# Stage C and the first batch's stage A on 64x64 quarters of TensorE, the combination's sums on VectorE, and a thinner hand-out of Fourier work in the first batch

## The chip, the cores and the metric

The kernel runs on one core of one Trainium2 chip. The core has five engines that work side by side: TensorE (PE in the profile, with its weight loads as PEld), VectorE (DVE), ScalarE (ACT), GpSimd (POOL) and SyncE (SP), which issues most of the DMAs. The metric is the time of one execution on the device in microseconds, the median of three runs.

## What is computed

Two things follow one another for 8 batches of 3008 rows with 256 columns.

```python
X = np.fft.rfft(x, axis=1)                       # along the 3008 rows
Yr = Xr @ w_r - Xi @ w_i + b_r                   # 256 x 256, complex
Yi = Xr @ w_i + Xi @ w_r + b_i
Yr = np.sign(Yr) * np.maximum(np.abs(Yr) - 0.01, 0)   # and the same for Yi
y = np.fft.irfft(Yr + 1j * Yi, n=3008, axis=1)
h = y.reshape(24064, 256) @ w_in                 # 256 x 2048
out = (h * np.cos(h)) @ w_out                    # 2048 x 256
```

## The kernel before

3008 is 64 x 47, so each transform is made of a 64-point one and a 47-point one, both as small matrix products. For a batch the Fourier part has these steps: **stage A** (the 64-point transform, `stage_a0` L410 for batch 0, `stage_a` L432 for the others), **stage B** (`stage_b` L522: the 47-point transform `forward` L557, the combination `combine` L581 that makes the three operands of a complex product, the product with the weights `wmix` L642, the soft threshold, and the inverse 47-point transform `inverse` L747), and **stage C** (`stage_c` L861, the inverse 64-point transform). Between them the data go through scratch tensors in DRAM (`scr1`, `scrF`, `scrT`, `scr2`), which turn them.

Behind it stands the second part, `moe_step` (L912) and `second` (L894), for six tiles of 512 rows (the last has 448) a batch and 16 steps a tile: `h` in six matmuls of 512 columns into a PSUM bank `ph` (L919 to L921; all large operands are split into a high part and a rest, so that three matmuls make one product), then ACT L928, DVE L929, ACT L931, DVE L932 for `u` = h cos h, ACT L934 for its high part `gh`, and the rest `gl` on POOL (L323, two steps in four) or DVE (L326). Three steps later six matmuls into `po` (L901, L902, L905) add up the product with `w_out`.

The Fourier part of batch b+1 is written as generators and is handed out between the steps of batch b. Every `yield` names a cost in units, and before and after the `po` matmuls of a step `pull` (L1046) takes pieces until the step's budget is used: `(C_COST + share(b)) / 15 / 2`. `share` (L1035) is the sum of the costs of a batch over 6 - SPREAD tiles, for batch 0 over 6 - 0.7 = 5.3, with `HEAD`, in which START, BT_WAIT and FIRST stand, added. START is the wait before the first loads of stage B of batch 1, FIRST the rest behind its first `forward`. At the head of each tile's pieces stands stage C of the next tile: loads of `bt`, a rest of BT_WAIT units, the matmuls, and a rest of BT_REST units. Before the whole loop runs a prologue (`first` L798), in which batch 0 goes through stages A and B alone.

Instructions are put in order per engine by a scheduler that follows a timeline of its own. `tc.issue_after(x)` forbids it to place an instruction before x. `floor()` (L315) does so for the last instructions of the step before the present one.

A matmul in single precision appears in the trace as two, each with a weight load of its own, and so does a call on a quarter. `burst` (L361) issues calls that use parts of the array of 64 x 64 (or 32 x 32) in one piece: the first call waits for everything, and the rest follow it without anything between them. Four calls that follow one another there take the four quarters: two halves of the input partitions, g, and two halves of the output partitions, v, with a PSUM bank for each g. So stage A of batches 1 to 7, `forward` and `spread` are made. Stage C and `stage_a0` use the whole array instead: 128 partitions hold two groups of 64 points, and their constants (`f1` and `ei` in `ff`, columns 0 to 127 and 128 to 255) are block-diagonal, so that each group meets its own block and the other block is zero.

- `stage_a0` (L410): six pieces of `x` are loaded, each 512 KB; for each half of a piece 4 calls of 128 columns write one bank, which ACT and DVE copy by turns.
- `stage_c` (L861): a tile has two halves `hf`; for each, 4 calls of 128 columns write one bank `pc`, ACT writes the high part `xTh` and DVE the rest `xTl`.
- `combine` (L581): for each part, ACT casts `Xh` (L592, L600, L607), DVE makes the rest `Xl` (L326, L593 and L602 call it), POOL adds the two parts of `z` (L599) and makes the last rest (L323).
- `stage_a(1)` runs its first three pieces in the prologue. The stores of the pieces 1 and 2 are held back (`held`, `release` L461) until the first matmuls `pc`.

## Time and profile before

| | us |
|---|---|
| median of 3 runs (2640.57 to 2641.7) | 2640.63 |
| the profiled execution's own time | 2643.39 |
| its span, first to last instruction | 2641.6 |
| TensorE busy in it | 2603.2 |
| VectorE, ScalarE, GpSimd busy | 1937.9, 1635.1, 979.1 |

The mean granted clock of TensorE is 0.995 of full. In the profile, a group of instructions is named by its line and engine, then the tile that it writes, an arrow and the tiles that it reads. "Idle before" is the time in which the engine had nothing to run just before an instruction, and the name behind it is what ended that. The end of a matmul is modelled, and matmuls overlap in the array, so that their pitch, from start to start, is what counts.

### The profile page before, as it was taken

The numbers are of one execution on the slowest core, as the hardware profiler recorded it, in microseconds if no ns is written. First come the engines' busy times: TensorE is split into PE (matmuls) and PEld (weight loads), VectorE is DVE, ScalarE is ACT, GpSimd is POOL, SyncE is SP. The second block draws the span as 40 slices with busy tenths as digits, with TensorE's granted clock in tenths as the row PEclk, the third lists the DMA queues.
The fourth block names the chain that finished last, engine by engine and source line by source line (L and its number), as shares of the span: only waits on it lengthen the run. The fifth ranks groups of instructions, "written<-read, shape, count | busy, mean of one in ns | idle before, by whom it ended". The sixth has DMA issues, their size and how long they took to land.

```text
span 2641.6 us, 38292 instructions
## 1 busy us (share of the span) xinstructions
PE 2603.2 (99%) x13657; PEld 2112.5 (80%) x13657; DVE 1937.9 (73%) x3089; ACT 1635.1 (62%) x3003; POOL 979.1 (37%) x946
## 2 busy tenths in 40 slices
PE   9899999999999999999999999999999999999999
PEld 7478778877788777887788877887778888888888
DVE  5797677878768777687776777677776778766665
ACT  5565556666666666656666666666666666566665
POOL 1224442444425453244533455234432433322222
PEclk9999999999999999999999999999999999999999
DMA  6535434344333444244433544235433343210000
GB/s 209 186 94 150 131 116 129 97 139 137 103 88 107 140 128 116 79 125 137 140 86 86 156 140 116 85 98 143 131 99 101 86 115 108 59 46 17 17 25 16
DMA packets 172935, 282.82 MB, mean 107 GB/s; under 512 B 15608, under 2 KB 114200, under 8 KB 169160
## 3 DMA queue, kind: packets, MB, share of 16 engines
q1 hardware_dynamic: 161896, 243.78, 32.8%
q0 software_dynamic: 10112, 35.53, 4.3%
q8 instruction: 108, 1.77, 0.3%
q10 hardware_dynamic: 736, 1.05, 0.1%
q14 instruction: 83, 0.68, 0.1%
HBM read 149.76 MB, written 130.55 MB: 106 GB/s over the span
## 4 chain that ended last, share of the span: by engine, by line
PE 88%; DVE 7%; ACT 2%; DMA 2%; issue 1%; POOL 1%; SPq 0%; ACTq 0%; DVEq 0%; POOLq 0%
PE ph L919 12%; PE po L901 12%; PE po L905 12%; PE po L902 12%; PE ph L920 12%; PE ph L921 12%; PE pc L881 3%; PE pw L658 2%; PE pw L659 2%; PE pw L660 2%; PE pb L375 1%; PE pw L654 1%; DVE u L932 1%; DVE u L929 1%; DVE Xl L326 1%
## 5 line engine op out<-in xcount | busy, mean ns | idle before, releaser
L323 POOL TENSOR_TENSOR gl<-u,gh 128x512 fp32r<-128x512 f32 (+1 forms) x384 | 502.6, 1309 | 1156.2 <-ACT gh L934 983.4
L931 ACT ACTIVATE u<-u 128x512 f32<-128x512 f32 (+1 forms) x768 | 478.6, 623 | 384.9 <-DVE u L929 383.7
L929 DVE SCALAR_TENSOR_TENSOR u<-ph,u 128x512 f32<-128x512 f32 (+1 forms) x768 | 514.5, 672 | 259.0 <-ACT u L928 257.8
L932 DVE TENSOR_TENSOR u<-ph,u 128x512 f32<-128x512 f32 (+1 forms) x768 | 518.1, 675 | 237.4 <-ACT u L931 226.7
L928 ACT ACTIVATE u<-ph 128x512 int32<-128x512 f32 (+1 forms) x768 | 448.0, 585 | 280.7 <-PE ph L921 271.2
L901 PE MATMUL po<-gh,wout 128*128 128x512 f32 (+1 forms) x1536 | 606.8, 395 | 13.3 <-ACT gh L934 13.1
L934 ACT CAST gh<-u 128x512 fp32r<-128x512 f32 (+1 forms) x768 | 467.9, 609 | 244.8 <-DVE u L932 241.1
L919 PE MATMUL ph<-xTh,win 128*128 128x512 f32 (+1 forms) x1536 | 606.7, 395 | 1.1 <-ACT xTh L886 0.7
L902 PE MATMUL po<-gh,wout 128*128 128x512 f32 (+1 forms) x1536 | 602.1, 392 | 0.0
L920 PE MATMUL ph<-xTl,win 128*128 128x512 f32 (+1 forms) x1536 | 597.3, 389 | 0.0
L921 PE MATMUL ph<-xTh,win 128*128 128x512 f32 (+1 forms) x1536 | 596.1, 388 | 0.0
L905 PE MATMUL po<-gl,wout 128*128 128x512 f32 (+1 forms) x1536 | 480.7, 391 | 0.5 <-POOL gl L323 0.5
L919 PEld LDWEIGHTS ph<-xTh,win 128*128 128x128 f32 x1536 | 289.6, 189 | 90.8 <-issue 20.8
L901 PEld LDWEIGHTS po<-gh,wout 128*128 128x128 f32 x1536 | 289.8, 189 | 79.7 <-ACT gh L934 18.6
L326 DVE TENSOR_TENSOR gl<-u,gh 128x512 fp32r<-128x512 f32 (+1 forms) x384 | 295.6, 770 | 66.9 <-ACT gh L934 59.0
L905 PEld LDWEIGHTS po<-gl,wout 128*128 128x128 f32 x1536 | 288.1, 189 | 66.9 <-issue 5.3
L921 PEld LDWEIGHTS ph<-xTh,win 128*128 128x128 f32 x1536 | 289.6, 189 | 57.5
L902 PEld LDWEIGHTS po<-gh,wout 128*128 128x128 f32 x1536 | 289.8, 189 | 54.6
L920 PEld LDWEIGHTS ph<-xTl,win 128*128 128x128 f32 x1536 | 289.8, 189 | 50.7 <-DVE xTl L887 0.4
L658 PE MATMUL pw<-Xh,wf 128*128 128x384 f32 x336 | 114.9, 342 | 2.0 <-ACT Xh L607 1.9
L659 PE MATMUL pw<-Xh,wf 128*128 128x384 f32 x336 | 114.0, 339 | 0.0
L660 PE MATMUL pw<-Xl,wf 128*128 128x384 f32 x336 | 111.8, 338 | 0.0
(121 smaller groups left out, 2468.5 us busy)
## 6 DMA issues: line engine op xcount, KB each, us to landing
scrF<-at SPq DMA_DIRECT2D x28, 1024.0 KB
z<-scrF SPq DMA_DIRECT2D x112, 256.0 KB
scrT<-tr SPq DMA_DIRECT2D x56, 512.0 KB
y<-scrT SPq DMA_DIRECT2D x112, 256.0 KB
bt<-scr SPq DMA_DIRECT2D x94, 256.0 KB
scr<-ao SPq DMA_DIRECT2D x84, 256.0 KB
scr<-bo SPq DMA_DIRECT2D x224, 96.0 KB
out_dram<-ob SPq DMA_DIRECT2D x80, 256.0 KB
```

What stands on the lines that cost most here:

```text
L323: return nc.gpsimd.tensor_tensor(out=lo, in0=x, in1=hi.bitcast(F32), op=ALU.subtract)
L901: mm(po[e][:, :n], wo[0][:, 0, f, es], gh[:, :n], start=f == 0, stop=False)
L902: mm(po[e][:, :n], wo[0][:, 1, f, es], gh[:, :n], start=False, stop=False)
L905: mm(po[e][:, :n], wo[0][:, 0, f, es], gl[:, :n], start=False, stop=f == NFC - 1)
L919: mm(h, win[:, 0, c, fs], th[:, c, :n], start=c == 0, stop=False)
L920: mm(h, win[:, 0, c, fs], tl[:, c, :n], start=False, stop=False)
L921: ins = mm(h, win[:, 1, c, fs], th[:, c, :n], start=False, stop=c == 1)
L928: nc.scalar.activation(k[:, :n], h, AF.Identity, bias=0.25, scale=1.0 / TWO_PI)
L929: nc.vector.scalar_tensor_tensor(out=u[:, :n], in0=h, scalar=1.0 / TWO_PI, in1=k[:, :n], op0=ALU.mult, op1=ALU.subtract)
L931: nc.scalar.activation(u[:, :n], u[:, :n], AF.Sin, bias=HALF_PI, scale=TWO_PI)
L932: product = nc.vector.tensor_tensor(out=u[:, :n], in0=h, in1=u[:, :n], op=ALU.mult)
L934: step = [nc.scalar.copy(gh[:, :n], u[:, :n])]
```

## The change

Stage C makes the same sums with 32 calls of 64 x 64 weights and 64 columns for a tile, one bank for each g, as one `burst` that waits for the loads of `bt`; the copies then go by g and no longer by half. The second tile of batch 0 rests 2.5 x BT_WAIT units between loads and matmuls. `stage_a0` makes its sums likewise, with 32 calls for a whole piece of `x`, kept together by the new `pinned`. In `combine` the sum of the parts of `z` is made by DVE instead of POOL, behind ACT's cast in the text; for batch 1 the three DVE operations have `floor(1)`, which names the last step instead of the one before. START is 6 instead of 12 and FIRST 24 instead of 36. In `stage_a(1)` the store of piece 0 is held back too.

```diff
@@ -46,7 +46,7 @@
 QUIET, READ, BURST, LAST = 3.0, 1.1, 2.5, 21.0
 BT_WAIT, BT_REST = 8.0, 2.0
 SPREAD, SPREAD_FIRST = 1.15, 0.7
-START, FIRST = 12.0, 36.0
+START, FIRST = 6.0, 24.0
 
 
 class Hold(float):
@@ -312,10 +312,10 @@
     mm = nc.tensor.matmul
     steps = []
 
-    def floor():
+    def floor(n=2):
 
         ctx = ExitStack()
-        for ins in steps[-2] if len(steps) > 1 else ():
+        for ins in steps[-n] if len(steps) > 1 else ():
             ctx.enter_context(tc.issue_after(ins.ins))
         return ctx
 
@@ -375,6 +375,12 @@
                 ins = mm(*a, **k)
         return ins
 
+    def pinned(calls):
+        ins = mm(*calls[0][0], **calls[0][1])
+        with tc.high_priority(), tc.issue_after(ins.ins):
+            for a, k in calls[1:]:
+                mm(*a, **k)
+
     def stage_out(name):
         return wk.tile([128, 1024], F32, tag="ao", name=name, bufs=3)
 
@@ -419,15 +425,17 @@
         load_fourier_w()
         load_f0(2)
         landed("x0", xs[5][:, :1])
-        for n in range(12):
-            p = fps("pa")
-            for c in range(2):
-                for i in range(2):
-                    o, k = 256 * c + 128 * i, 512 * (n % 2) + 256 * i + 128 * c
-                    mm(p[:, o:o + 128], xs[n // 2][:, k:k + 128], ff[:, :128], start=o == 0, stop=o == 384,
-                       skip_group_check=True)
-            mark["dve"] = mark["a0", n % 2] = (nc.vector.tensor_copy if n % 2 else nc.scalar.copy)(
-                a0[0][:, :, 2 * n:2 * n + 2], p.rearrange("p (c i k) -> p c i k", c=2, i=2))
+        for n in range(6):
+            p = [fps("pa") for _ in range(2)]
+            pinned([((p[g][64 * v:64 * v + 64, 256 * c + 64 * i:256 * c + 64 * i + 64],
+                      xs[n][64 * g:64 * g + 64, 256 * i + 128 * c + 64 * v:256 * i + 128 * c + 64 * v + 64],
+                      ff[64 * g:64 * g + 64, :128].rearrange("p (r g s) -> p g r s", r=2, g=2)[:, g]),
+                     dict(start=c == 0 and i == 0, stop=c == 1 and i == 3, skip_group_check=True))
+                    for i in range(4) for c in range(2) for v in range(2) for g in range(2)])
+            for g in range(2):
+                mark["dve"] = mark["a0", g] = (nc.vector.tensor_copy if g else nc.scalar.copy)(
+                    a0[0][:, :, 4 * n:4 * n + 4].rearrange("p c i (r g s) -> p g c i r s", r=2, g=2)[:, g],
+                    p[g].rearrange("p (c i r s) -> p c i r s", c=2, i=4, r=2))
 
     def stage_a(b):
         scr1[b] = dr.tile([2, 24, 32, 2, 256], F32, tag="scr1", name=f"scr1_{b}")
@@ -484,7 +492,7 @@
                     drained(p[c, h], nc.scalar.copy(ao[:, 512 * h:512 * h + 512], p[c, h]))
                     if h == 0 or c < cs[-1]:
                         yield Hold(READ)
-                if pro and c:
+                if pro:
                     held.append((c, ao))
                 else:
                     store(c, ao)
@@ -591,15 +599,16 @@
                 with floor():
                     nc.scalar.copy(hi[0][:, v], z[:, 0, v])
                 yield 0.8
-                with floor():
+                with floor(1 if b == 1 else 2):
                     rest(lo[0][:, v], z[:, 0, v], hi[0][:, v])
                 yield 0.9
             for v in range(2):
                 with floor():
-                    nc.gpsimd.tensor_tensor(out=z[:, 0, v], in0=z[:, 0, v], in1=z[:, 1, v], op=ALU.add)
                     nc.scalar.copy(hi[1][:, v], z[:, 1, v])
+                with floor(1 if b == 1 else 2):
+                    nc.vector.tensor_tensor(out=z[:, 0, v], in0=z[:, 0, v], in1=z[:, 1, v], op=ALU.add)
                 yield 0.9
-                with floor():
+                with floor(1 if b == 1 else 2):
                     rest(lo[1][:, v], z[:, 1, v], hi[1][:, v])
                 yield 1.2
             for v in range(2):
@@ -865,26 +874,28 @@
 
         bt = wk.tile([128, 4, 256], F32, tag="bt", name="bt", bufs=1)
         first = b == 0 and t == 0
+        loads = []
         for h in range(0, 4, 2 if first else 4):
             m = 2 if first else 4
             for g in range(2):
                 n0 = 24 * g + 4 * t + h
-                ((nc.scalar, nc.gpsimd)[g] if first else nc.sync).dma_start(
-                    bt[64 * g:64 * g + 64, h:h + m], scr2[b][n0:n0 + m].rearrange("i r s d -> (r s) i d"))
-        yield BT_WAIT
-        for hf in range(2):
-            p = fps("pc")
-            with tc.issue_after(mark["pa"].ins) if b == 0 and t == 0 else floor() if b == 0 and t == 1 else ExitStack():
-                for j in range(2):
-                    for c in range(2):
-                        o = 256 * j + 128 * c
-                        ins = mm(p[:, o:o + 128], bt[:, 2 * hf + j, 128 * c:128 * c + 128], ff[:, 128:256], start=o == 0, stop=o == 384,
-                                 skip_group_check=True)
-            mark.setdefault("pc", ins)
-            pv = p.rearrange("p (j c n) -> p c j n", j=2, c=2)
-            thv, tlv = (a[:, :, 256 * hf:256 * hf + 256].rearrange("p c (j n) -> p c j n", j=2) for a in (th, tl))
+                loads.append(((nc.scalar, nc.gpsimd)[g] if first else nc.sync).dma_start(
+                    bt[64 * g:64 * g + 64, h:h + m], scr2[b][n0:n0 + m].rearrange("i r s d -> (r s) i d")))
+        yield 2.5 * BT_WAIT if b == 0 and t == 1 else BT_WAIT
+        p = [fps("pc") for _ in range(2)]
+        with tc.issue_after(mark["pa"].ins) if b == 0 and t == 0 else floor() if b == 0 and t == 1 else ExitStack():
+            ins = burst(2, [((p[g][64 * v:64 * v + 64, 256 * c + 64 * i:256 * c + 64 * i + 64],
+                              bt[64 * g:64 * g + 64, i, 128 * c + 64 * v:128 * c + 64 * v + 64],
+                              ff[64 * g:64 * g + 64, 128 + 64 * g:192 + 64 * g]),
+                             dict(start=c == 0 and i == 0, stop=c == 1 and i == 3, skip_group_check=True))
+                            for i in range(4) for c in range(2) for v in range(2) for g in range(2)],
+                        () if first else loads)
+        mark.setdefault("pc", ins)
+        for g in range(2):
+            pv = p[g].rearrange("p (c i m) -> p c i m", c=2, i=4)
+            thv, tlv = (a.rearrange("p c (i g m) -> p g c i m", i=4, g=2)[:, g] for a in (th, tl))
             nc.scalar.copy(thv, pv)
-            drained(p, nc.vector.tensor_tensor(out=tlv, in0=pv, in1=thv.bitcast(F32), op=ALU.subtract))
+            drained(p[g], nc.vector.tensor_tensor(out=tlv, in0=pv, in1=thv.bitcast(F32), op=ALU.subtract))
         yield BT_REST
 
 
```

## Rows read from the trace of the kernel before

**Rows 1.** The profile's page: busy time of each engine, its share of the span and its instructions; and, from another part, the chain of work that ended last, by engine.

```profile
PE 2603.2 (99%) x13657; PEld 2112.5 (80%) x13657; DVE 1937.9 (73%) x3089; ACT 1635.1 (62%) x3003; POOL 979.1 (37%) x946
...
PE 88%; DVE 7%; ACT 2%; DMA 2%; issue 1%; POOL 1%; SPq 0%; ACTq 0%; DVEq 0%; POOLq 0%
```

**Rows 2.** Who TensorE waited for, over the whole span: the waiting engine and line, what it waited for, us in total, times, the longest.

```profile
PE po L901 <- ACT gh L934: 13.1, 8, 4.8
...
PE pw L658 <- ACT Xh L607: 1.9, 5, 0.4
```

**Rows 3.** The same view from 130 to 440 us.

```profile
PE po L901 <- ACT gh L934: 12.4, 6, 4.8
PE pc L881 <- DVE u L932: 1.8, 1, 1.8
PE pc L881 <- DMA bt<-scr: 1.7, 1, 1.7
PE pi L365 <- DMA y<-scrT: 1.3, 1, 1.3
```

**Rows 4.** Busy time by stretch: from and to in us, length, then for PE, PEld, DVE, ACT and POOL the busy us and (instructions), then the granted clock, the DMA share and GB/s.

```profile
130.00:160.00 30.00, 26.11 (x134) 20.46 (x135) 28.13 (x47) 18.77 (x34) 6.82 (x6) 0.94 0.35 95
...
280.00:300.00 20.00, 15.15 (x56) 12.22 (x56) 15.54 (x24) 11.20 (x22) 10.45 (x9) 0.83 0.35 90
...
340.00:360.00 20.00, 15.77 (x61) 12.69 (x60) 18.67 (x27) 10.31 (x21) 11.27 (x10) 0.83 0.24 74
```

**Rows 5.** Groups of instructions of one shape over the whole span: count, busy us, mean ns of one, idle us before them.

```profile
L881 PE MATMUL pc<-ff,bt 128*128 128x128 f32 x768 | 100.0, 278 | 7.2 <-DMA bt<-scr 5.4 <-DVE u L932 1.8
```

**Rows 6.** TensorE's timeline around one tile of stage C: start in us, how long the row lasts, line, output and inputs, instructions in the row.

```profile
957.48 1.95 PE L881 MATMUL pc<-ff,bt 128*128 128x128 f32 x16
959.18 0.47 PE L919 MATMUL ph<-xTh,win 128*128 128x512 f32 x1
959.50 0.39 PE L920 MATMUL ph<-xTl,win 128*128 128x512 f32 x1
959.73 0.40 PE L921 MATMUL ph<-xTh,win 128*128 128x512 f32 x1
```

**Rows 7.** TensorE's timeline around one burst of stage B on quarters.

```profile
608.58 0.40 PE L902 MATMUL po<-gh,wout 128*128 128x512 f32 x1
608.91 0.43 PE L365 MATMUL pb<-at,fq 48*64 48x256 f32 x1
...
609.18 0.38 PE L365 MATMUL pb<-at,fq 48*64 48x256 f32 x1
609.18 1.68 PE L375 MATMUL pb<-at,fq 48*64 48x256 f32 x27
610.80 0.50 PE L919 MATMUL ph<-xTh,win 128*128 128x512 f32 x1
611.14 0.40 PE L920 MATMUL ph<-xTl,win 128*128 128x512 f32 x1
```

**Rows 8.** The weight loads at the head of that burst.

```profile
608.91 0.13 PEld L365 LDWEIGHTS pb<-at,fq 48*64 48x64 f32 x1 [0.37 <-DVE u L932]
...
608.96 0.13 PEld L365 LDWEIGHTS pb<-at,fq 48*64 48x64 f32 x1
```

**Rows 9.** Busy time by stretch of TensorE alone (us, (instructions), clock, DMA share, GB/s), for the first 0.15 us of a burst of the inverse that came after a wait of 1.26 us for its data.

```profile
417.39:417.54 0.15, 0.12 (x16) 1.00 0.00 0
```

**Rows 10.** Groups of one shape again: the combination's rests on DVE, the last subtraction of the threshold on DVE, and the sums on POOL.

```profile
L326 DVE TENSOR_TENSOR Xl<-z,Xh 128x384 fp32r<-128x384 f32 x112 | 104.5, 962 | 8.9 <-ACT Xh L592 6.4 <-ACT Xh L600 2.1
...
L684 DVE TENSOR_TENSOR st<-st,cl 128x384 f32<-128x384 f32 x122 | 83.3, 686 | 1.2
...
L599 POOL TENSOR_TENSOR z<-z 128x384 f32<-128x384 f32 x56 | 69.5, 1255 | 24.8 <-DVE Xl L326 24.8
```

**Rows 11.** DVE's timeline around the long stall of batch 0 (in brackets the idle time before a row and what ended it).

```profile
273.99 0.45 DVE L715 STREAM_TRANSPOSE tr<-odd 128x256 f32<-128x256 f32 x1 [5.90 <-POOL odd L707]
...
281.88 1.45 DVE L326 TENSOR_TENSOR Xl<-z,Xh 128x384 fp32r<-128x384 f32 x1
283.25 0.54 DVE L684 TENSOR_TENSOR st<-st,cl 128x384 f32<-128x384 f32 x1
```

**Rows 12.** POOL's timeline before and in it.

```profile
266.85 1.59 POOL L448 TENSOR_TENSOR xe<-xt 128x512 f32<-128x512 f32 x1 [4.20 <-DMA xt<-in_dram]
...
271.13 1.29 POOL L449 TENSOR_TENSOR xt<-xt 128x512 f32<-128x512 f32 x1
...
283.41 1.25 POOL L599 TENSOR_TENSOR z<-z 128x384 f32<-128x384 f32 x1 [0.49 <-DVE Xl L326]
...
285.48 1.33 POOL L599 TENSOR_TENSOR z<-z 128x384 f32<-128x384 f32 x1
```

**Rows 13.** The first 20 us by stretch, columns as in rows 4.

```profile
0.00:20.00 20.00, 15.97 (x103) 14.57 (x103) 4.54 (x7) 5.00 (x8) 6.82 (x18) 0.91 0.89 262
```

**Rows 14.** The timelines of the start, one row each of TensorE, POOL and DVE.

```profile
6.75 12.61 PE L427 MATMUL pa<-ff,x 128*128 128x128 f32 x96 [1.95 <-DMA ff<-in_dram]
...
17.14 0.19 POOL L403 COPY seen<-x 128x1 f32<-128x1 f32 x1 [9.97 <-DMA ws<-in_dram]
...
19.40 0.69 DVE L429 COPY a<-pa 128x512 f32<-128x512 f32 x1 [1.09 <-PE pa L427]
```

**Rows 15.** The chain of work that ended last, from 100 to 115 us: start, us, what.

```profile
105.52 3.73 DMA bt<-scr
```

## The prediction

> **What bounds the kernel now.** I read the page's engine table and its chain of waits first. TensorE is busy 2603 of 2641.6 us and the chain runs through it for 88% of the span; DVE has 73% and POOL 37% [rows 1]. Then I read who TensorE waits for: 13.1 us for the cast `gh`, and, once in most batches, some tenths for `Xh`, 1.9 us in all [rows 2]. So after the start TensorE works almost without a pause, and only work taken from it shortens the span. [...] Batch 0 thus has 17.2 + 8.6 = 25.8 us that are no PE work.
>
> **Stage C (48 tiles).** Now: 8 calls, which the profile shows as 768 / 48 = 16 matmuls of 128 columns [rows 5]. In a tile that lies between plain matmuls the 16 start at 957.48 and the next one at 959.18, and that one holds the array 0.32 us where its kind takes 0.23 [rows 6]: 1.70 + 0.09 = 1.79 us, a pitch near 0.111. Half of what each multiplies are the zeros of the block-diagonal `ei`.
>
> After: 32 calls on 64x64 quarters, 64 matmuls of 64 columns in 16 groups of four. The nearest rows are the bursts that already run on quarters. Stage B's has 16 calls, 32 matmuls of 256 columns, 8 groups [rows 7]. Its second group starts at 609.18, and from there 1 + 27 matmuls, seven groups, last until 609.18 + 1.68 = 610.86; less the 0.38 of the last, six group steps took 1.28 us after the offset of 0.02 within a group: 0.214 each. Four quarters truly run together. Around the burst, the mode costs time: the plain matmul before started at 608.58 and should hold 0.23, but the burst starts at 608.91 (0.10 lost); the first group takes 0.27, not 0.214 (0.05: its weights load uncovered); the last group should be done at 610.68, the next plain matmul starts at 610.80 and holds 0.34 instead of 0.23 (0.12 + 0.11). Together 0.38, I take 0.37 a burst.
>
> The pitch of a group at 64 columns no row shows. From below: a quarter's second weights load 608.96 - 608.91 = 0.05 us after its first [rows 8]; and 64 columns at the pace of rows 6 are 0.111 / 2 = 0.056, as is what the first group of rows 7 is longer. From above: no gain from halving the columns, 0.111. [...] Issuing is no limit either: after a wait that had emptied the queue, 16 quarter calls started within 0.15 us [rows 9], 0.009 each; stage C wants one per 0.029.
>
> So a tile costs 16 x 0.058 + 0.37 = 1.30 us against 1.79: 0.49 saved. The first tile hangs on DMA; 47 x 0.49 = 23.0 us. With 0.05 it is 29, with 0.075 it is 10.
>
> The copies out of PSUM stay two on ACT and two on DVE a tile, but both banks now end together. Nothing waits for them, a tile being transformed long before its first `ph`; only at the very first tile do ACT's two copies follow one another where one ran beside the second half's matmuls: -0.5 to +0.6 us, nothing taken.
>
> [...]
>
> **The combination's sums.** 56 additions of 1.255 us leave POOL (70 us) and go to DVE. What one takes there no row shows; 128x384 with two SBUF operands takes DVE 0.686 on average (`st`) and 0.962 (`Xl`) [rows 10], so 38 to 54 us; I take 0.69, as for the same kind without a cast. DVE rises to about 75%. While a POOL sum runs, an `Xl` on DVE takes 1.45 us, where the similar `st` takes 0.54 [rows 11]; that goes. So for each sum DVE has 0.69 more and up to 0.9 less: nothing in the steady batches, where TensorE covers it. Queued behind the sum on DVE are `u` L929 and L932; `gh` waits for these, and `po` for `gh`. If that cover is thin, one step in each of seven batches comes 0.7 late: +5 us. If `Xh` comes earlier, the 1.9 us of rows 2 go: -2.
>
> **The first batch.** Four edits act here. START and FIRST leave 18 units fewer to hand out, so share(0) falls by 18 / 5.3 = 3.4 units and the work comes about 5% thinner; `bt` of the second tile gets 20 units to land, not 8; the sums leave POOL; DVE's part of the combination stays behind the last step, not the one before. The long stall shows what they meet: `xt` lands late, POOL works through four `xe`/`xt` operations from 266.85 on [rows 12] before it makes `odd`; DVE stands 5.90 us at `tr`, which waits for that `odd` [rows 11]; two POOL sums (1.25 and 1.33) then delay the next half's `odd` [rows 12]; DVE works off a backlog, and `po` gets `gh` 4.8 us late [rows 3]. The sums' 2.6 us go from that stall and from the like one near 355 (TensorE busy 15.77 of 20 us [rows 4]): 5.2. One of the two clock losses goes with it: 3.4. The wait for `bt`, 1.7 [rows 3], goes by the longer rest. The sums cost DVE some 1 us of it. I take 9 of the 25.8. Bounds: all of it gone, or 8 us more, if the new order makes one more stall with its clock loss (4.8 + 3.4).
>
> **The start.** The mean clock is 0.91 of full over the first 20 us [rows 13]. Stage A of batch 0 has 96 matmuls from 6.75 to 19.36 and its last copy from 19.40 to 20.09 [rows 14]; as quarters it has 96 groups x 0.058 = 5.6 us of work. But POOL's `seen`, which waits for the last piece of `x`, runs only at 17.14 [rows 14] (the row names `ws`, but by the code it is the piece of `x` that it reads); only then can the sixth burst start: 17.14 + 0.93 + 0.2 (last matmul to copy, as now) + 0.69 = 18.96, 1.1 us earlier. [...] I take 0; bounds -1.1 and +2. Stage A(1)'s first store now waits for the first `pc`: its two DMAs are no longer in flight beside the 3.73 us of `bt` [rows 15], up to 0.7 sooner. Later, the second tile's loads stand behind two more issues on SP, with 20 units to spare. Nothing taken.
>
> **Sum.** The profiled execution took 2643.39 us, 1.8 outside the span of 2641.6. 2643.4 - 23.0 - 9 = 2611.4. The median of the three runs, 2640.63, is 2.8 below the profiled one: 2608.6.
>
> **Rivals.**
> 1. Stage C gains, batch 0 doesn't: the stalls only move, since DVE is busy 28.13 of 30 us there [rows 4] and gets more to do. 2640.6 - 23 = 2617.6; with one new stall, 2626. For it: that DVE load. Against: in the long stall DVE itself was waiting for POOL.
> 2. Slower: in a quarter the load isn't hidden. Place: every stage C burst. Price: a group takes load and matmul, 0.056 + 0.058 = 0.114, a tile 16 x 0.114 + 0.37 = 2.19, 0.40 more than now; 47 of them +18.8, less 9: 2650. It decides from a pitch of (1.79 - 0.37) / 16 = 0.089 on for stage C, and of 0.10 for the whole change. [...] Against: rows 7, and the plain pitch of rows 6.
> 3. All stalls of batch 0 go: 2640.6 - 23 - 25.8 = 2592.
> 4. The pitch comes near 0.089, so the quarters give nothing: batch 0's part alone or not even that, 2632 to 2641.
>
> **How the numbers follow.** Forecast 0.62; rival 1 0.20; rival 2 0.06; rival 3 0.08; rival 4 0.04. Two tenths of a per cent, 5.3 us, is about what a measurement of this kernel can tell from no change. Faster: 0.62 + 0.20 + 0.08 + half of rival 4 = 0.92; same 0.02; slower 0.06. Range 2594 to 2627: down to pitch 0.05 with two thirds of batch 0's loss gone, up to rival 1 with its new stall.
>
> **What would show it.** Right: `pc` as 3072 matmuls, and about 1.30 us from the first of a tile to the next plain one, switches included; PE busy down by some 23 us; waits for `gh` between 130 and 440 us under 8 us; no dip of the clock in at least one of 280 to 300 and 340 to 360. Wrong: groups of four more than 0.07 apart; a wait of `po` for `gh` in every batch after 480 us; the clock down behind stage A at the start; `pc` of the second tile waiting for `bt` again.

## The result, and the profile after

The changed kernel takes 2664.94 us (2662.49 to 2667.44) where the kernel before took 2641.16 on the same chip: 1.0088 of it, with an interval of 1.0076 to 1.0101, so 23.8 us slower where 32 us faster had been forecast. The profiled execution took 2662.49 us, 1.8 outside its span.

The page of the changed kernel, the lines that answer to [rows 1]:

```profile
span 2660.7 us, 43519 instructions
PE 2590.4 (97%) x16249; PEld 2069.3 (78%) x16249; DVE 1945.2 (73%) x3145; ACT 1632.5 (61%) x3003; POOL 912.3 (34%) x890
...
PE 83%; DVE 10%; ACT 3%; DMA 2%; issue 2%; POOL 0%; SPq 0%; DVEq 0%; ACTq 0%; POOLq 0%
```

TensorE is busy 12.8 us less, but the span is 19.1 us longer: it has less to do and waits more. DVE's total hardly moved (1937.9 to 1945.2 us), yet its share of the chain rose from 7% to 10%: VectorE is not fuller, it stands in the way at more places.

Where the 19.1 us came from I read off TensorE's timeline, from one batch's first `po` to the next. Before, the first `po` of batch 1 came at 478.3 us, after at 486.5: +8.2. Batches 1 to 5 took 318.1, 317.3, 317.8, 317.5 and 319.5 us, and now 322.9, 320.0, 321.3, 320.3 and 322.6: +16.9. Batch 6, which has no stage A of a later batch beside it, went from 308.5 to 305.0, and the rest from 264.6 to 262.2: -5.9. So stage C's saving of 6 x 0.49 = 2.9 us a batch shows only at the end, where least is handed out beside the second part.

TensorE's waits from 480 us on, first of the kernel before, then of the changed one (who waited, for whom, us in total, times, the longest):

```profile
PE pw L658 <- ACT Xh L607: 1.9, 5, 0.4
PE po L901 <- ACT gh L934: 0.7, 2, 0.4
```

```profile
PE po L912 <- ACT gh L945: 15.5, 14, 2.2
PE ph L930 <- DVE u L943: 4.8, 6, 1.4
PE pw L667 <- DVE u L943: 1.6, 5, 0.3
PE po L916 <- POOL gl L323: 0.9, 5, 0.2
```

`po` almost never waited for `gh` in these batches; now it does 14 times. The longest, 2.2 us, comes once in each of the batches 1 to 5, in the fourth tile, where the combination runs. In four of the five a spell of 3.41 us at 0.50 of the full clock goes with it: behind 991.6 us, in batch 2, the mean granted clock is 0.59 until 995.7, 1.7 us lost. In batches 1 to 5 TensorE's waits thus rose from 2.6 to 22.8 us and the clock's loss from 0 to 6.8, while stage C has some 15 us less to do; that leaves 4 or 5 of the 16.9 us open.

The stretches of batch 0 that [rows 4] show, and the one behind stage A of the start, after the change (columns as there):

```profile
130.00:160.00 30.00, 25.04 (x162) 18.70 (x155) 29.16 (x43) 18.39 (x34) 10.59 (x8) 0.94 0.57 174
280.00:300.00 20.00, 19.25 (x113) 14.74 (x112) 15.91 (x25) 8.76 (x16) 11.62 (x10) 1.00 0.42 141
340.00:360.00 20.00, 20.00 (x117) 15.76 (x116) 14.23 (x22) 11.04 (x21) 10.52 (x10) 1.00 0.49 144
...
20.00:40.00 20.00, 17.12 (x131) 14.93 (x131) 7.40 (x16) 10.10 (x22) 2.10 (x4) 0.76 0.69 256
```

The two stalls near 290 and 355 us are gone, with their clock losses. But others have come. Three of TensorE's four largest waits from 130 to 440 us, after the change:

```profile
PE pi L365 <- DMA y<-scrT: 5.4, 1, 5.4
...
PE po L912 <- ACT gh L945: 4.5, 5, 2.2
PE pb L365 <- issue: 3.9, 1, 3.9
```

All waits there add up to 23.4 us (18.1 before). With the `pi` that waits for `y` until 431.05 and the `pb` that stops until 206.1 go spells at 0.50 of the full clock too, from 429.1 to 435.9 and from 207.2 to 210.7 us; the clock's loss between 130 and 440 us is 6.8 us (8.5 before). So the stalls of batch 0 moved.

From 20 to 40 us the mean granted clock is 0.76, where it was 1.00 before: 20 x 0.24 = 4.8 us lost. Over the first 20 us it is 0.99, where it was 0.91 [rows 13]; over both together the start loses 3.4 us more than before.

TensorE's timeline around one tile of stage C, which answers to [rows 6]:

```profile
970.66 0.63 PE L916 MATMUL po<-gl,wout 128*128 128x512 f32 x2
971.22 0.27 PE L365 MATMUL pc<-ff,bt 64*64 64x64 f32 x1
...
971.33 1.05 PE L375 MATMUL pc<-ff,bt 64*64 64x64 f32 x59
972.31 0.50 PE L930 MATMUL ph<-xTh,win 128*128 128x512 f32 x1
972.64 0.40 PE L931 MATMUL ph<-xTl,win 128*128 128x512 f32 x1
```

The two `po` hold 0.46 us, so the burst starts 0.10 late; it is 1.09 to the next `ph`, which holds 0.33 where its kind takes 0.23. Together 1.29 us, forecast 1.30. This part of the prediction was right, and it gained nothing in batches 1 to 5.

VectorE in the fourth tile of batch 2, in the changed kernel (start, us, what), ahead of a wait of 2.20 us that TensorE ends at 991.61:

```profile
985.85 0.67 DVE L326 TENSOR_TENSOR gl<-u,gh 128x512 fp32r<-128x512 f32 x1
986.44 0.55 DVE L326 TENSOR_TENSOR Xl<-z,Xh 128x384 fp32r<-128x384 f32 x1
986.91 0.55 DVE L609 TENSOR_TENSOR z<-z 128x384 f32<-128x384 f32 x1
987.38 2.93 DVE L326 TENSOR_TENSOR Xl<-z,Xh 128x384 fp32r<-128x384 f32 x2
990.23 0.68 DVE L943 TENSOR_TENSOR u<-ph,u 128x512 f32<-128x512 f32 x1
```

The same place in the kernel before:

```profile
973.01 2.32 DVE L326 TENSOR_TENSOR Xl<-z,Xh 128x384 fp32r<-128x384 f32 x3
975.26 0.68 DVE L932 TENSOR_TENSOR u<-ph,u 128x512 f32<-128x512 f32 x1
```

`u` now stands behind four instructions of the combination, 990.23 - 986.44 = 3.79 us; before, behind three, 975.26 - 973.01 = 2.25 us. The sum itself takes 0.55 us here (0.62 on average over all 56), less than the 0.69 that I took; the two `Xl` behind it take 1.46 each.

That is 1.5 us more, and the wait is 2.2: TensorE's own order has changed there too. The wait in the changed kernel, and the same `po`, of the sixth step of the fourth tile, in the kernel before, each with the `ph` nearest to it:

```profile
991.61 0.50 PE L912 MATMUL po<-gh,wout 128*128 128x512 f32 x1 [2.20 <-ACT gh L945]
...
993.57 0.63 PE L930 MATMUL ph<-xTh,win 128*128 128x512 f32 x1
```

```profile
980.02 0.39 PE L921 MATMUL ph<-xTh,win 128*128 128x512 f32 x1
...
982.01 0.39 PE L901 MATMUL po<-gh,wout 128*128 128x512 f32 x1
```

Before, this `po` stood behind the `ph` of two more steps and the `pw` between them, and its `gh` had ended 5.4 us ahead of it. Now it stands ahead of them, right behind the `po` of the step before. It is so in each of the batches 1 to 5.

And the start: TensorE in stage A of batch 0, two rows of the changed kernel (in brackets the idle time before; "issue" means that nothing which the profile shows held it):

```profile
14.72 0.81 PE L382 MATMUL pa<-ff,x 64*64 64x64 f32 x41 [1.90 <-issue]
...
22.01 1.24 PE L382 MATMUL pa<-ff,x 64*64 64x64 f32 x37 [5.20 <-issue]
```

Both stops lie inside a burst, whose first call had already waited for its piece of `x`. Nothing of the kind stood in [rows 14].

### The profile page after: what moved, and what is told of

Its sections match the earlier page's. It is cut to its first block, busy times and chain, and to the rows that moved or that the text cites. A ratio compares the mean times of both kernels' runs of the same rounds, so it can differ in the third digit from the quotient of the medians.

```text
span 2660.7 us, 43519 instructions
## 1 busy us (share of the span) xinstructions
PE 2590.4 (97%) x16249; PEld 2069.3 (78%) x16249; DVE 1945.2 (73%) x3145; ACT 1632.5 (61%) x3003; POOL 912.3 (34%) x890
## 4 chain that ended last, share of the span: by engine, by line
PE 83%; DVE 10%; ACT 3%; DMA 2%; issue 2%; POOL 0%; SPq 0%; DVEq 0%; ACTq 0%; POOLq 0%
PE ph L930 12%; PE po L912 12%; PE po L913 11%; PE ph L931 11%; PE ph L932 11%; PE po L916 11%; PE pw L667 2%; PE pw L668 2%; PE pw L669 2%; DVE u L943 2%; DVE u L940 1%; DVE Xl L326 1%; PE pc L375 1%; PE pb L375 1%; PE pw L663 1%
## 5 line engine op out<-in xcount | busy, mean ns | idle before, releaser
L943 DVE TENSOR_TENSOR u<-ph,u 128x512 f32<-128x512 f32 (+1 forms) x768 | 517.8, 675 | 237.5 <-ACT u L942 225.1
L939 ACT ACTIVATE u<-ph 128x512 int32<-128x512 f32 (+1 forms) x768 | 449.0, 587 | 328.5 <-PE ph L932 316.1
L930 PE MATMUL ph<-xTh,win 128*128 128x512 f32 (+1 forms) x1536 | 606.0, 395 | 10.6 <-DVE u L943 9.3
L931 PE MATMUL ph<-xTl,win 128*128 128x512 f32 (+1 forms) x1536 | 597.9, 389 | 0.1
L930 PEld LDWEIGHTS ph<-xTh,win 128*128 128x128 f32 x1536 | 290.3, 189 | 101.9 <-DVE u L943 19.1
L326 DVE TENSOR_TENSOR gl<-u,gh 128x512 fp32r<-128x512 f32 (+1 forms) x384 | 287.4, 748 | 72.8 <-ACT gh L945 68.8
L931 PEld LDWEIGHTS ph<-xTl,win 128*128 128x128 f32 x1536 | 290.5, 189 | 51.6 <-DVE xTl L898 0.6
L716 POOL TENSOR_TENSOR odd<-st 128x184 f32<-128x184 f32 (+1 forms) x112 | 69.2, 619 | 137.9 <-DVE st L693 135.2
```

The lines of the kernel that those rows point to most:

```text
L930: mm(h, win[:, 0, c, fs], th[:, c, :n], start=c == 0, stop=False)
L931: mm(h, win[:, 0, c, fs], tl[:, c, :n], start=False, stop=False)
L939: nc.scalar.activation(k[:, :n], h, AF.Identity, bias=0.25, scale=1.0 / TWO_PI)
L943: product = nc.vector.tensor_tensor(out=u[:, :n], in0=h, in1=u[:, :n], op=ALU.mult)
```

## The experiments

Three theories stood at first. S: the sums on VectorE make `gh` late. F: stage A on quarters makes the start late. B: stage C's saving is lost because TensorE, faster there, meets work that is no faster.

**e1_sum_pool: the sums back on POOL.**

```diff
-nc.vector.tensor_tensor(out=z[:, 0, v], in0=z[:, 0, v], in1=z[:, 1, v], op=ALU.add)
+nc.gpsimd.tensor_tensor(out=z[:, 0, v], in0=z[:, 0, v], in1=z[:, 1, v], op=ALU.add)
```

> The changed kernel with one edit: the combination's sum is made by POOL again, at the same place in the text. Theory S (the sum on DVE is what costs the steady batches, some 6.5 us in each of six, and part of batch 0): 2632 to 2640 us, and the wait of po for gh near 992 us with its clock dip is gone. Rival B (stage C's burst, with both banks ready at once and nothing in between, makes u and gh late): it stays at 2660 or above, with the same waits.

2636.82 us, 0.9977 of before (0.9968 to 0.9986): 28.1 us less than the changed kernel. The sums are its largest loss.

**e2_a0_whole: stage A of batch 0 on whole weights, as before; the rest as changed.**

> The changed kernel with stage A of batch 0 on the whole array as before. Theory F (384 small matmuls run TensorE out of loaded instructions, two pauses of 1.9 and 5.2 us in the middle of a burst): the pauses are gone, the first transposes start near 20.2 instead of 24.3 us, and the time falls by 4 to 6 us to 2659 to 2661. Rival X (the pauses are waits for pieces of x): the start is no earlier and the time stays within 1 us.

2656.35 us, 1.0051 (1.0036 to 1.0066): 8.6 us less than the changed kernel, more than the 4 to 6 expected. The stops are gone, the first transposes run at 19.8 us instead of 24.3.

**e3_stage_c_only: the kernel before with stage C on quarters, nothing else.**

> The kernel before with stage C on quarters as the only edit (BT_WAIT as before for all tiles). Theory S: the 0.49 us of each tile come off the span, 2641 - 23 = 2618 (2612 to 2624), and no new waits from 480 us on. Rival B: 2640 to 2650, with waits of po for gh in every batch.

2641.33 us, 0.9996 (0.9986 to 1.0005). The burst is as short as in the changed kernel, and the time is the same as before. From 480 us on, `po` now waits 10.5 us for `gh`, ten times; batches 1 to 5 take 316.9 to 319.3 us, as before.

**e4_sum_dve_only: the kernel before with the sums on VectorE, nothing else.** In the text the sum stays ahead of ACT's cast, where the change has it behind.

> The kernel before with the combination's sum on DVE as the only edit. Theory S: 2641 plus 20 to 30, with a wait of po for gh of some 2 us and a clock dip in every steady batch. Rival B: within 4 us of 2641.

2661.33 us, 1.0069 (1.0054 to 1.0084): 18.3 us slower by this alone, with a wait of 2.2 us in the fourth tile of each of the batches 1 to 5, and 12.3 us of waits for `gh` from 480 us on. TensorE's `po` there has moved up as in the changed kernel.

**e5_pool_whole: e1 and e2 together,** so that stage C and the hand-out are left of the change.

> The changed kernel with the combination's sums back on POOL and stage A of batch 0 on whole weights, so stage C on quarters and the thinner hand-out stay. If the two losses found so far add up (the sums 28 us, stage A0's pauses 8.6 us) it takes 2636.8 - 8.6 = 2628 us (2624 to 2632), steady batches as without the VectorE sums (about 315 to 318 us), first transposes at 20 us. If the pause of the start is made up again in batch 0 once the sums are on POOL (a stall there ends later for another reason), it stays at 2635 to 2638.

2638.98 us, 0.9981 (0.9972 to 0.9991). The two gains did not add up. Batch 1 starts 6.9 us earlier than in e1 (480.5 to 487.4), but batches 1 to 5 took 7.0 us longer in the profile. The two run the same instructions there, but not in quite the same order: ScalarE's differs at 22 of 1820 places, VectorE's at 6 of 1901. ScalarE at the head of the fourth tile of batch 2, first in e1, then in e5 (L939 and L937 are the first instruction of a step, the others the cast `gh`):

```profile
966.08 0.58 ACT L939 ACTIVATE u<-ph 128x512 int32<-128x512 f32 x1
966.93 0.62 ACT L945 CAST gh<-u 128x512 fp32r<-128x512 f32 x1 [0.28 <-DVE u L943]
```

```profile
960.93 0.62 ACT L943 CAST gh<-u 128x512 fp32r<-128x512 f32 x1 [0.76 <-DVE u L941]
961.46 0.59 ACT L937 ACTIVATE u<-ph 128x512 int32<-128x512 f32 x1
```

In batch 2 e1 then waits 0.3 us for `gh` and takes 314.9 us, e5 waits 2.2 and takes 318.7; batch 4 is like it (314.9 and 319.3). In batches 1, 3 and 5 e1 is within 0.8 us of e5, with the same two orders at this place, so it is not this swap alone. In the totals, stage A's 8.6 us show only with the sums on VectorE.

**e6_handout: the kernel before with the thinner hand-out alone,** the `floor(1)` of batch 1 and the held store of piece 0 included (not shown).

```diff
-START, FIRST = 12.0, 36.0
+START, FIRST = 6.0, 24.0
...
-        yield BT_WAIT
+        yield 2.5 * BT_WAIT if b == 0 and t == 1 else BT_WAIT
```

> The kernel before with the thinner hand-out of the first batch alone (START 6, FIRST 24, the second tile's stage C later, the combination of batch 1 bound to the last step instead of the one before, the first two raw stores held). If the hand-out is what took the two long stalls of batch 0 away, the stalls near 290 and 356 us (4.8 and 5.5 us) go also here and batch 0 ends some 8 to 13 us earlier: 2629 to 2635 us, steady batches 317 to 320 us as before. If it only works with a shorter stage C, or moves the stalls elsewhere in batch 0, 2640 to 2646 us.

2635.51 us, 0.9976 (0.9966 to 0.9986): 6.0 us less. The stalls near 290 and 355 us are gone; batch 1 starts at 467.1 us instead of 478.3 in the profile.

**e7_skew4 and e8_before_skew4: `po` one step further behind `ph`,** in e5 and in the kernel before, to give `gh` more time. Room is made by one `fq` buffer instead of two, two `kc` buffers instead of three (not shown) and by keeping `ident` for the prologue alone.

```diff
-SKEW = 3
+SKEW = 4
...
-                fq = wk.tile([128, 512], F32, tag="fq", name="fq", bufs=2)
+                fq = wk.tile([128, 512], F32, tag="fq", name="fq", bufs=1)
```

> The same as the run with POOL sums and whole stage A0, and po one step further behind ph (SKEW 4 for 3; room made by one fq buffer and two kc buffers). Cover theory: stage C's saving of 0.49 us a tile is lost in the steady batches because gh ends just as its first po matmul could start in one or two steps of each batch; with one step more (about 2.6 us) between them the waits of po for gh after 480 us go (under 1 us in all), every steady batch falls to 3 us under its length before (314.5 to 316.5 us where it was 317.3 to 319.5), and the whole takes 8 to 14 us less than the run with SKEW 3, about 2617 us. Rival, the bound lies elsewhere (weight loads, the clock, another wait that comes in its place): the time stays within 3 us of the SKEW 3 run or rises.

> The kernel before with SKEW 4 and the same room made, nothing else. Cover theory: before, the steady batches' waits of po for gh are small (some 1 us a batch), so that they gain no more than 1 to 2 us each; batch 0's long stalls (4.8 and 5.5 us) shrink by up to 2.6 us each: 2628 to 2638 us. What the SKEW 4 run of the changed kernel is then ahead of this one is stage C's 23 us and the hand-out: 15 to 25 us. Rival (the bound lies elsewhere): 2641 to 2645 us.

2658.76 us, 1.0065 (1.0050 to 1.0080), and 2661.80 us, 1.0069 (1.0053 to 1.0086): both some 20 us slower, a miss of the cover theory. The first of the waits of e7 from 480 us on:

```profile
PE po L908 <- ACT ob L916: 29.2, 9, 3.7
```

`gh` came in time (1.1 us in all), but the first `po` of a tile now waits for `ob`, the copy that frees the accumulators. That copy is ScalarE's too. In all nine it runs right behind ScalarE's casts of the combination or instructions of later steps, 5.0 to 7.1 us after the `po` that it copies have ended (1.0 in the median tile). So the wait moved to the next thing that TensorE needs from ScalarE. Whether the distance or the smaller buffers brought the new order was not separated.

**e9_evict_first: e5, and the next step's first ScalarE and VectorE instruction bound behind stage C's evictions.**

> POOL sums, whole stage A0, stage C on quarters, and the next step's first ScalarE and VectorE instruction bound behind stage C's evictions (xTh, xTl). With stage C on quarters the evictions were seen to end 3 to 7 us after the burst where they ended 1 to 3 us after it before, because the order puts them behind the next step's work on both engines. Eviction theory: the late evictions and the work bunched behind them push u and gh of the combination's steps back and so take stage C's 0.49 us a tile back; with them first, the last xTl ends under 3 us after the burst in every tile, the waits of po for gh at 598, 657, 975, 1234, 1293, 1612 us go (under 2 us in all after 480), the steady batches fall to 314 to 316 us and the whole to 2622 to 2630 us. Rival, the combination's own chain is the bound in these steps whatever the order of the evictions: 2636 to 2642 us, waits as before. Bound both: the evictions now wait for the burst with a step's work behind them, and a new wait of ph for u costs up to 0.5 us a tile, 2645 to 2660 us.

2636.73 us, 0.9978 (0.9969 to 0.9988). Inconclusive: the order of all engines came out as in e5, because the `ph` that TensorE runs behind the burst belongs to a step that is written before it. The evictions in the fourth tile still ended 5.3 to 7.1 us after the burst. What it shows is how far runs of one order differ: the medians are 2.2 us apart (on two chips), single executions of e5 alone 10.9 (2629.70 to 2640.55), and single waits for `gh` come and go by up to 1.4 us.

**e10_rest_dve: the changed kernel with the combination's last `Xl` on VectorE too.**

```diff
-                    rest_pool(lo[2][:, v], z[:, 0, v], hi[2][:, v])
+                    rest(lo[2][:, v], z[:, 0, v], hi[2][:, v])
```

> The changed kernel with the last rests of the combination (Xl of the third part) on VectorE too, so that POOL does nothing in the combination. Contention theory: the sums on VectorE cost because POOL, freed of them, runs its own Xl at the same time as VectorE's, and VectorE's then take 1.46 us for 0.55; without POOL all of VectorE's Xl and z take 0.55 to 0.7, two more of them cost 1.1 to 1.4 us, and the combination's run on VectorE gets no longer: the wait of 2.21 us in each batch shrinks and the time falls to 2645 to 2658 us. Occupancy theory: what costs is the number of VectorE instructions ahead of u: two more of them make the wait longer by 1.1 us or more in each batch, 2668 to 2680 us.

2658.32 us, 1.0061 (1.0044 to 1.0078): more work on VectorE, and no slower. The median is 6.6 us less, but the executions of the two overlap (2654.64 to 2664.13, and 2662.49 to 2667.44). So the amount of VectorE's work alone does not decide; by it 2668 us or more were expected. What POOL runs beside them is part of it by these rows: the two `Xl` behind the sum take 2.12 us here, while POOL runs `gl`, against 2.93 in the changed kernel, where POOL runs `gl` and an `Xl` of its own from 987.33 to 989.89 us.

**e11_a0_half: stage A of batch 0 on quarters for three of its six pieces.**

> The changed kernel with the first three pieces of stage A0 on quarters and the last three on whole weights (494 instead of 782 TensorE records up to the transposes). Instruction theory: TensorE stops after the same number of its own records as in the changed kernel, 445 (weight loads and matmuls together), which now lies in the whole pieces, for 1 to 2 us, right after an instruction packet has landed; the second stop, after 699, falls behind the first transposes, which start at 20 to 22 us. Rival, the stops come from the quarters' banks and copies: they stay within the first three pieces, at the same matmul of a piece as before, or both go. Time beside the changed kernel: 4 to 9 us less, about 2658 us.

2657.17 us in one execution; the transposes start at 20.7 us. Neither picture came exactly: there is no stop "by issue" at all. Counted in the trace, the two stops of the changed kernel lie behind the 445th and the 699th record of TensorE, weight loads included, and so they do in e1 and e10, at other times. Each ends 1.3 to 1.6 us after a 16,384-byte packet of the instruction queue has landed (13.26 then 14.72, and 20.73 then 22.01 in the changed kernel). In e11 that packet had landed at 14.18, and TensorE waited for `x` until 15.59 anyway. That fits instructions running out, and does not prove it.

At this point e3's ScalarE told more than its waits. ScalarE around stage C of the fourth tile of batch 2, first in e3, then in the kernel before (L930 and L928 are the step's first instruction, k; L933 and L931 the Sin; L936 and L934 the cast `gh`):

```profile
959.79 0.63 ACT L933 ACTIVATE u<-u 128x512 f32<-128x512 f32 x1 [2.80 <-DVE u L931]
961.18 0.62 ACT L936 CAST gh<-u 128x512 fp32r<-128x512 f32 x1 [0.76 <-DVE u L934]
961.70 0.59 ACT L930 ACTIVATE u<-ph 128x512 int32<-128x512 f32 x1
963.05 0.63 ACT L933 ACTIVATE u<-u 128x512 f32<-128x512 f32 x1 [0.76 <-DVE u L931]
964.45 0.62 ACT L936 CAST gh<-u 128x512 fp32r<-128x512 f32 x1 [0.76 <-DVE u L934]
964.97 1.06 ACT L888 CAST xTh<-pc 128x512 fp32r<-128x512 f32 x2
```

```profile
958.08 0.63 ACT L931 ACTIVATE u<-u 128x512 f32<-128x512 f32 x1 [2.81 <-DVE u L929]
958.62 0.58 ACT L928 ACTIVATE u<-ph 128x512 int32<-128x512 f32 x1
959.47 0.62 ACT L934 CAST gh<-u 128x512 fp32r<-128x512 f32 x1 [0.27 <-DVE u L932]
960.07 0.63 ACT L931 ACTIVATE u<-u 128x512 f32<-128x512 f32 x1
960.60 1.05 ACT L886 CAST xTh<-pc 128x512 fp32r<-128x512 f32 x2
```

Before, k of the next step runs ahead of `gh` of this one at this place (it does so in 57 to 60 of the 96 steps of a batch), and while VectorE works on one step ScalarE works on the other. In e3 the order is Sin, `gh`, k, Sin, `gh`: one step after the other, 0.76 us idle at each hand-over, and the evictions of a burst that ended near 960 run at 964.97. The order that the scheduler writes had moved when stage C changed. In e3 `xTh` had its data 4.9 us before it ran: the burst's last matmul ends at 960.07, and ScalarE ran `gh`, k, Sin and `gh` first. That made a fourth theory, O: what takes the gains back is the order, and it can be pinned.

**e13_defer: e5 with `gh` of a step issued behind k of the next.**

```diff
+    def finish(first=None):
...
+            with tc.issue_after(first.ins) if first else ExitStack():
+                step = [nc.scalar.copy(gh[:, :n], u[:, :n])]
...
-        nc.scalar.activation(k[:, :n], h, AF.Identity, bias=0.25, scale=1.0 / TWO_PI)
+        first = nc.scalar.activation(k[:, :n], h, AF.Identity, bias=0.25, scale=1.0 / TWO_PI)
+        finish(first)
...
-        step = [nc.scalar.copy(gh[:, :n], u[:, :n])]
...
+        late.append((u, gh, gl, n, f, product))
```

`floor` then names the last finished step for all batches, so that the `floor(1)` of batch 1 is gone with it. The pin holds for every step, also for the 36 to 39 of a batch in which the kernel before has `gh` first.

> POOL sums, whole stage A0, stage C on quarters, and the order of ScalarE pinned: gh of a step is issued behind the first ScalarE instruction (k) of the next step, so that the chains of two steps always overlap. Order theory: with stage C on quarters the order that was written for ScalarE ahead of stage C of the fourth tile runs two steps one after the other (k, Sin, gh, k, Sin, gh, idle 0.76 us at each hand-over to VectorE) where before they overlapped (k, Sin, k, gh, Sin, gh), and so the evictions end 5 to 7 us after the burst there, against 2 to 3 us, and po waits for gh right behind. Pinned, the last xTl ends under 4 us after the burst in the fourth tile, the waits of po for gh of 1.8 us there go, the steady batches fall by 1.5 to 3 us each (to 315 to 316.5 us) and the whole to 2624 to 2632 us. Rival, it is not the order but the amount of VectorE work in the combination: waits stay, 2635 to 2642 us; or gh, now later in every step, turns late elsewhere: above 2642 us.

2627.49 us, 0.9950 (0.9935 to 0.9965): 11.5 us less than e5 (8 by the ratios, the two being from different chips). The evictions in the fourth tile end 1.96 us after the burst, and the waits for `gh` from batch 1 on fall from 9.8 to 1.1 us. Some of it returns as waits for `gl`, 5.7 us.

**e14_late_quarters: e5 with stage C on quarters from batch 1 on.**

> The thinner hand-out with stage C on quarters from batch 1 on, and on whole weights as before in batch 0 (POOL sums, whole stage A0). Batch 0 ended at 467 us with the hand-out alone and at 480 us with quarters too (a wait of 6.9 us of ph for u at 132 us behind the preparation of weights on VectorE, waits at 199 and 299 us). If the quarters of batch 0 bring these waits, batch 0 ends at 465 to 470 us, batch 7 and the tail keep 305 and 262.2 us, and the whole takes 2624 to 2631 us. If the waits come with any change of the order there, batch 0 ends at 475 to 482 us and the whole takes 2634 to 2641 us.

2629.99 us, 0.9959 (0.9944 to 0.9974): 9.0 us less than e5 by the medians, 6 by the ratios, whose intervals touch. The wait of 6.9 us near 132 us is gone: with quarters there, VectorE ran six instructions of the weights' preparation in a row ahead of `u` (122.5 to 129.8 us). Batch 1 starts at 472.9 us, 7.6 earlier, though not at the 465 to 470 expected.

**e15_z_spread: the changed kernel with a rest between the casts and the sums.**

```diff
                     nc.scalar.copy(hi[1][:, v], z[:, 1, v])
+                yield 0.9
                 with floor(1 if b == 1 else 2):
```

The planned sum of a batch's costs, `COST`, is raised by the rests added, 4 x 1.8 units (not shown), so that the pace of the hand-out rises with it.

> The changed kernel with one more rest of 0.9 between the combination's second casts and its sums on VectorE (and the plan's total raised by the same), so that the sum and the Xl behind it come a step apart where the two came together. Bunching theory: what costs 18 to 28 us is that z and two slowed Xl stand in one row ahead of one u (4.0 us of VectorE where it was 2.3); spread, the waits of 2.21 us of each steady batch fall under 1 us, and the whole to 2640 to 2652 us. Rival, VectorE's total work or its contention with POOL decides: 2658 to 2668 us.

2643.92 us, 1.0009 (0.9999 to 1.0018): 21.0 us less, with the same work on VectorE. The sum is not always apart: in the fourth tile of batch 2 a sum and two `Xl` still stand in one row, from 985.40 to 989.49 us, but the last `u` L944 of the sixth step runs ahead of it, `gh` starts at 985.54, and that step's `po` does not wait. So it is not the work that costs, but what stands behind it.

**e16_late_defer: e13 and e14 together.**

> Quarters from batch 1 on, and gh behind the next step's k, together. If both theories hold the gains add: batch 0 near 467 us, steady batches 315 to 316.5 us, 2613 to 2622 us. If only one holds, 2624 to 2632 us; if gh turns late elsewhere, above 2635 us.

2616.65 us, 0.9907 (0.9891 to 0.9924). Four of the batches 1 to 5 take 315.2 to 315.4 us in the profile, the fifth 320.5: it has the wait of 2.9 us below and 1.7 us of lower clock behind it. ScalarE at the same place as above (L967 is k, L971 the Sin, L943 `gh`):

```profile
941.83 0.63 ACT L971 ACTIVATE u<-u 128x512 f32<-128x512 f32 x1 [1.39 <-DVE u L969]
942.37 0.58 ACT L967 ACTIVATE u<-ph 128x512 int32<-128x512 f32 x1
943.22 0.62 ACT L943 CAST gh<-u 128x512 fp32r<-128x512 f32 x1 [0.27 <-DVE u L972]
943.82 0.63 ACT L971 ACTIVATE u<-u 128x512 f32<-128x512 f32 x1
944.58 1.07 ACT L911 CAST xTh<-pc 128x512 fp32r<-128x512 f32 x2
```

At this place it is the order of the kernel before, with the short burst. All of TensorE's waits from 470 us on in this run:

```profile
PE po L930 <- POOL gl L324: 2.9, 1, 2.9
PE po L926 <- ACT gh L943: 1.2, 5, 0.2
```

**e17_defer_whole: the hand-out alone (e6) with the order pinned,** so that it differs from e16 by stage C's quarters, and by the sum standing ahead of the cast in the text.

> The control for stage C: the hand-out alone (stage C on whole weights in all tiles, 2635.5 us) with gh behind the next step's k, as in the 2616.7 us version, from which it differs by stage C's quarters of batches 1 to 7. Order theory: whole weights lost nothing to the order (no wait of po for gh in the steady batches), so pinning it gains little: 2630 to 2636 us, steady batches 317 to 318.5 us, and the 2616.7 us version is then 14 to 19 us ahead, near the 42 x 0.49 = 20.6 us that stage C was to bring. Rival, the pinned order is worth its gain by itself: 2620 to 2626 us, and stage C's quarters bring under 10 us.

2636.45 us, 0.9972 (0.9962 to 0.9982): pinning brings nothing where stage C is on whole weights (2635.51 without). Stage C's quarters are therefore worth 2636.45 - 2616.65 = 19.8 us in batches 1 to 7, where 42 x 0.49 = 20.6 were to come. The two are from different chips; by the ratios, 0.9972 and 0.9907, it is 17 us, by the spans of the two profiles 18.8.

**e18_best_sum_dve: e16 with the sums on VectorE,** as the change has them.

> The 2616.7 us version with the combination's sums on VectorE, as the change has them. Bunching theory: with the order pinned, gh has its margin in the combination's steps, and 1.1 us more of VectorE a combination costs little: 2616 to 2624 us. Rival, the sums cost by VectorE's amount of work ahead of u whatever ScalarE's order: 18 us or more on top, 2632 to 2645 us.

2614.64 us, 0.9890 (0.9876 to 0.9905). The move that cost 18.3 us in e4 costs nothing here. From 470 us on `po` does not wait for `gh` at all:

```profile
PE po L930 <- POOL gl L324: 6.7, 8, 1.2
```

The intervals of e16 and e18 overlap; both beat the kernel before and the changed one.

## Why the prediction was wrong

**Stage C.** The tile was right: 1.29 us against the 1.30 forecast, groups 0.058 apart, 2976 + 96 = 3072 matmuls. No row of the kernel before shows the 0.058 that the sum takes for a group; it was an estimate, and the changed kernel showed the same in its place. For the whole-array calls of before the trace has 0.19 us for a load and 0.28 for a matmul, both at one pitch. The second rival, loads in series in a quarter, falls: by it the groups would have been 0.114 apart. What failed is the step from the tile to the kernel, "47 x 0.49 = 23.0 us": alone, the edit brought nothing (e3). It counted TensorE's time and kept the order of all engines as it was, while that order is written anew with each change. e17 and e16 show the saving, 17 to 20 of 20.6 us, once the order is pinned.

**The sums.** The step that failed is "nothing in the steady batches, where TensorE covers it", with +5 as its bound. Alone they cost 18.3 us (e4), in the change 28.1 (e1). I had the duration a little too high (0.69, measured 0.62 on average). The relief, "that goes", was a misreading: the `Xl` of 1.45 us in [rows 11] did not run beside a sum. The sum waited for it until 283.41 [rows 12]; beside it POOL ran a `gl`, from 281.51 to 282.92. So a POOL subtraction goes with a slow `Xl` as well, and without the sums POOL runs its own `Xl` and `gl` there, and the two `Xl` take 1.46 us each; over the whole span the mean `Xl` fell only from 0.96 to 0.86 us. The cover was not looked at step by step. In the trace of before, in four of the 96 steps of each of the batches 1 to 5 (one in the first tile, one in the third, two in the fourth), `gh` ends only 0.05 to 0.83 us before its first `po` starts, where the median step has some 5 us; the waits, 0.7 us in all, do not show that. The waits of e3 are at two of these four. But the wait of 2.2 us, with the sums on VectorE, is at a step that had 5.4 us: there TensorE's `po` moved up and met a `u` that was 1.5 us later. e15 and e18 show that the order costs, not the work: with one more rest ahead of the sums 21 us come back, with the order pinned all. In e18 that `po` stands as far up, and does not wait.

**The first batch.** -9 was forecast, out of 25.8: the waits of [rows 3], 17.2 us, and what the three stretches of [rows 4] lack of full clock, 8.6. In the trace of before these stretches hold spells at 0.50 of the full clock, of 3.41, 6.83 and 6.83 us; half of 6.83 is the 3.4 of one clock loss. The hand-out alone brings 6.0 (e6), and both stalls went as described. But in the changed kernel batch 1 starts 8.2 us later, and the waits between 130 and 440 us are 23.4 us instead of 18.1: the first rival's "the stalls only move" came. What failed is the step that took the sums' time on POOL, the wait for `bt` and one clock loss off the stalls and put at nothing the new ones that the new order makes, other than as a bound. Quarters in batch 0 are part of it (e14 is 6 to 9 us ahead of e5), by a wait near 132 us that no rival had: VectorE's order again, with the preparation of weights ahead of `u`.

**The start.** 0 was taken, with +2 as the upper bound, which no run shows; it cost 8.6 us (e2). I had asked when data would land, and not what else can stop TensorE: 768 records instead of 192 up to the transposes, and two stops among them. That issuing is no limit was read from [rows 9], and there from 16 records of 8 calls, not 16 calls; stage A's two stops come behind 445 and 699. In e1 and e5, with the sums on POOL, the loss does not show in the total. The clock behind it, named as a sign of being wrong, did fall: 0.76 from 20 to 40 us.

**The signs.** Of those set down, the right ones came (3072 matmuls, 1.29 us, `gh` waits of 4.5 us between 130 and 440 us, no dip at 280 to 300 and 340 to 360), except that PE's busy time fell by 12.8 us and not by 23. Two of the wrong ones came as well: `po` waiting for `gh` in every one of the batches 1 to 5, and the clock down behind stage A. The mechanism that I gave the slower side, a weight load not hidden, was not the one that came. The versions with a pinned order, 2614.6 and 2616.7 us, lie in the range forecast, but they have whole weights in batch 0: the terms of work were about right from batch 1 on, and the order was left out.

**What stays open.** Why the pinned order is not found by the scheduler itself was not looked into. The pin changes TensorE's and VectorE's order as well as ScalarE's; which of them gives the gain was not separated. That e5 and e9 run one order and still differ in single waits for `gh` (1.26 and 0.23 us in the third tile of batch 1) isn't explained. That the stops of the start are instructions not yet loaded is the reading that fits best; no run shows it alone.

## What to carry to other kernels

Where orders are written by a scheduler, a saving on the bounding engine can change the order of all engines: compare these orders around the edit, the bounding engine's own included, and read the smallest margin of the result that is handed back, not its mean. If a saving is measured on the tile and missing from the whole, look for idle gaps of one hand-over (here 0.76 us) in a chain that used to overlap, and pin the overlap before undoing the edit. More distance between producer and consumer may only move such a wait to the next thing that the other engine frees, as in e7.

## What the hardware showed that was not expected

TensorE stopped inside dense bursts of small matmuls, with nothing in the profile that held it. The stops of 1.90 and 5.20 us stand 254 records apart, and each ends 1.3 to 1.5 us after a 16,384-byte packet of the instruction queue has landed, which fits instructions running out. No run shows it alone.

Taking a sum of 1.26 us off POOL did not free VectorE's rests from POOL: its other instructions ran beside them, and two rests took 1.46 us each, where the one ahead of them took 0.55.
